# Polysketch attention followed by a rational-Padé feed-forward: keys in nine tiles of four, the first loads regrouped, one bank for the key-value products, and a new order of steps

## The chip, the cores and the metric

The kernel runs on one core of a Trainium2 chip. The metric is device time in microseconds (us): 277.58 us is the median of three runs (276.32 to 277.84). Beside these there is one profiled execution, whose trace is read below. The core has a matrix engine (TensorE, PE in the profile), a vector engine (VectorE, DVE), a scalar engine (ScalarE, ACT), GpSimd (POOL) and SyncE (SP), which here only issues DMA transfers. Each engine takes its instructions strictly in program order and waits on semaphores for what other engines and the transfers have to deliver.

## The reference, cut to what matters

Two stages. The first is a linear attention over 4 batches, 4 heads, 1088 tokens and head size 32, with two sketch matrices `S1` and `S2` of 8 x 32. The second is a feed-forward over all 4352 tokens (128 to 2048 to 128) with a rational function in the middle.

```python
def phi(x):
    a = einsum('rd,bhsd->bhsr', S1, x); b = einsum('rd,bhsd->bhsr', S2, x)
    return einsum('bhsi,bhsj->bhsij', a, b).reshape(..., 64)
q_p, k_p = phi(q), phi(k)
kv = einsum('bhsf,bhsd->bhfd', k_p, v); z = sum(k_p, axis=2)
x = einsum('bhsf,bhfd->bhsd', q_p, kv) / (einsum('bhsf,bhf->bhs', q_p, z) + 1e-6)

h = x @ w_in                                  # x as 4352 x 128
P = a0 + a1*h + a2*h**2 + a3*h**3
Q = 1 + |b0|*|h| + |b1|*h**2
out = (P / (Q + 1e-6)) @ w_out
```

The sums over tokens in `kv` and `z` take tokens in any order, so how the tokens of `k` and `v` are dealt out to tiles is free as long as both are dealt out alike.

## The kernel before, in words

**The table.** The program is a list of small steps. `ORDER` holds `name:index` entries; the loop at its end calls one method for each, and that call issues the instructions of the step, on one engine mostly. So the table sets the order on every engine at once, and nothing rearranges it later. Three loads are steps too: `lk`, `lv`, `lq` fetch the keys, values and queries of a later batch. All loads of batch 0 and of the weights are issued before the table begins.

**Keys.** For each batch, `Keys` makes `kv` and `z`. The 1088 tokens of a head lie as 32 groups of `NJ` = 34 tokens, one group to a partition, four heads on 128 partitions. `kt` (`transposes`) turns 32 x 32 blocks on VectorE so that a tile of 128 columns holds 4 x 32 tokens; `ks` (`sketches`) multiplies each tile by both sketch matrices on TensorE; `kc` (`copies`) takes one of the two results out of PSUM on ScalarE; `kf` (`features`) makes the 64 products on VectorE; `kp` (`products`) accumulates them against `v` and a column of ones on TensorE; `kk` (`keep`) copies the sums to `kvz` on ScalarE. Before, 34 = 4 * 8 + 2: eight full tiles (`NT`, `NM` = 8, 4) and a ninth of 64 tokens, in two parts of 4 and 5 tiles, with three transposes (512, 512 and 64 columns), and a `v` that takes six loads a batch: four of 128 KB and two of 16 KB.

**Queries.** `qt`, `qs`, `qc`, `qf`, `qp`, `qd`, `qi`, `qx`, `qb`, `qk` do a block of up to 384 queries: transposes, sketches, copies, features, products against `kvz`, denominator, its inverse, quotient, transposition back, and the copy to `xT`. Blocks 0 to 2 (batch 0) keep all on the chip. Blocks 3 to 12 (`Spread`) send their sketches through DRAM to spread them over partitions: `qc` copies them to `sk_sb`, then SP writes `sk_d` and reads back `a_all` and `b_all`, and `qf` on VectorE waits for that.

**Feed-forward.** Seventeen units of 4096 columns. Unit 0 is the first 256 tokens against all 16 blocks of hidden rows; each later tile of 512 tokens is two units. Of a unit, `h0` to `h3` are its hidden matmuls (TensorE, two PSUM tiles of 1024 columns in turn), `e0` to `e3` their copies to bf16 on ScalarE, `u`, `w`, `y` make Q on VectorE, `ln` and `ex` its reciprocal `r` on ScalarE, `pa` or `pd` the upper part of P on ScalarE or VectorE, `s`, `m`, `x` on VectorE build `h*r` and the rest, `G` multiplies by `w_out`, and `st` stores. `w_out` exists in three bf16 copies, made by six steps `wo:0` to `wo:5` (two halves of rows each); five ran on ScalarE and one on VectorE. Unit 0's `h2` and `h3` stand first in the table, and they need hidden blocks 8 to 15, the upper half of `w_in`. A step `tn` issues matmuls on an idle tile that produce nothing used.

**What stands around the change.** SP issues in program order; a load that waits for its buffer, or for room in the queue, holds all behind it. `k_sb` and `v_sb` have a single buffer: `lk:1` waits for the transposes of batch 0, `lv:1` for its products. PSUM has four banks for the attention (`bank`) and two tiles of two banks for the hidden layer (`wide`).

Of the kernel before, what the change touches and what calls it, by code (L numbers as in the profile page):

```python
# [11 lines left out]
FP = mybir.dt.float32  # L12
# [7 lines left out]
TURNS = (12, 2, 2, 2, 2, 2)  # L20
ORDER = """
tn:3 tn:0 kt0:0 kt2:0 kt1:0 ks0:0 qt:0 ba:0 tn:4 qt:1 kc0:0 tn:5 kf0:0 ks1:0 lk:1 qs:0 kc1:0 kf1:0 qc:0 kp0:0 qf:0
kp1:0 lv:1 qs:1 kk:0 qt:3 qc:1 qp:0 qt:2 qf:1 qs:3 qd:0 qs:2 qi:0 qx:0 qc:2 lq:1 qf:2 qp:1 qc:3 qb:0 qp:2 qd:1 qk:0
qi:1 qx:1 h2:0 wo:0 qd:2 wo:3 qi:2 qx:2 wo:4 h3:0 e2:0 wo:2 kt1:1 qb:1 h1:0 kt2:1 kt0:1 e3:0 wo:1 u1:0 ks1:1 w1:0
pa1:0 lk:2 qt:5 ks0:1 qt:4 qs:5 y1:0 h0:0 kc0:1 qk:1 kc1:1 wo:5 kf0:1 e1:0 kf1:1 qb:2 qs:4 qk:2 e0:0 h1:1 qt:6 ln1:0
qf:3 lq:2 u0:0 h2:1 w0:0 qc:4 ex1:0 kt0:2 tn:2 y0:0 qp:3 e2:1 s1:0 kp0:1 ln0:0 kt1:2 kp1:1 kt2:2 qt:7 m1:0 qd:3 e1:1
h0:1 qi:3 ex0:0 qx:3 x1:0 h3:1 e0:1 s0:0 kk:1 lk:3 h2:2 m0:0 lv:2 e3:1 pa0:0 u1:1 h3:2 w1:1 e2:2 ks0:2 y1:1 e3:2 h0:2
pa1:1 h1:2 qf:4 e0:2 x0:0 qp:4 kc0:2 qc:5 e1:2 kf0:2 ln0:1 ks1:2 pd0:1 u1:2 tn:1 qb:3 qd:4 G0:0 ex0:1 qi:4 w1:2 G1:0
qx:4 G2:0 qk:3 s0:1 kc1:2 ln1:1 qb:4 G3:0 y1:2 G4:0 qk:4 ex1:1 G5:0 kf1:2 qs:7 h2:3 ln0:2 qt:8 s1:1 h3:3 e2:3 m0:1
ex0:2 m1:1 h0:3 kt1:3 e3:3 qf:5 G0:1 s0:2 qs:8 qc:7 e0:3 h1:3 ln1:2 x0:1 st:0 h0:4 m0:2 e1:3 pa0:2 u1:3 h1:4 qt:9 w1:3  # L30
e0:4 G1:1 ex1:2 x1:1 h3:4 y1:3 e1:4 qp:5 e3:4 h2:4 x0:2 qd:5 ln0:3 lq:3 s1:2 qs:6 e2:4 G2:1 qi:5 pd1:2 ex0:3 G3:1 qx:5
u1:4 G4:1 G5:1 pa0:3 m1:2 qb:5 w1:4 G0:2 ln1:3 G1:2 qf:7 G2:2 m0:3 G3:2 qk:5 qc:6 ex1:3 x1:2 G4:2 h0:5 pd0:4 pa1:3
y1:4 h2:5 e0:5 qt:11 v0:3 ln0:4 kp0:2 s0:3 h3:5 m1:3 e2:5 ex0:4 x0:3 h1:5 v1:3 e3:5 kp1:2 s1:3 e1:5 s0:4 lv:3 h1:6
ln1:4 u1:5 h2:6 m0:4 e1:6 ex1:4 w1:5 G5:2 h0:6 kt0:3 kk:2 qf:6 e2:6 y1:5 G0:3 pa1:4 G2:3 h3:6 s1:4 ln0:5 st:2 qp:7
x1:3 e0:6 m1:4 qp:6 ex0:5 x0:4 G3:3 qc:8 s0:5 e3:6 G5:3 qd:7 ks0:3 qd:6 pa0:5 u1:6 G0:4 qi:6 qx:6 G1:4 qi:7 ln1:5 qx:7
G2:4 x1:4 qb:7 G3:4 w1:6 ex1:5 G4:4 m0:5 qb:6 qk:7 G5:4 qk:6 s1:5 pa0:6 qs:9 h0:7 y1:6 pa1:5 h1:7 kt2:3 m1:5 e0:7 G0:5
v0:5 kc0:3 e1:7 m0:6 h2:7 ln0:6 qf:8 h3:7 x1:5 qc:9 e2:7 st:4 qp:8 x0:5 e3:7 ex0:6 u1:7 ks1:3 h3:8 qt:10 w1:7 qd:8
ln1:6 qi:8 h1:8 y1:7 e3:8 kc1:3 ex1:6 G2:5 kf1:3 h0:8 e1:8 pd1:6 kf0:3 ln0:7 qs:10 h2:8 s1:6 e0:8 s0:6 G3:5 ex0:7 G4:5
m1:6 G5:5 qf:9 G0:6 qx:8 qc:10 e2:8 ln1:7 s0:7 qb:8 kp0:3 u1:8 kp1:3 qk:8 ex1:7 v0:6 G0:7 w1:8 h3:9 pa0:7 x0:6 y1:8
h2:9 kk:3 e3:9 G2:6 e2:9 s1:7 h1:9 ln0:8 m0:7 x1:6 h0:9 e1:9 m1:7 ex0:8 h0:10 x0:7 e0:9 u1:9 G3:6 ln1:8 pd1:7 G4:6  # L40
u0:9 G5:6 s0:8 e0:10 qp:9 qf:10 ex1:8 w1:9 qp:10 x1:7 pa0:8 h2:10 m0:8 w0:9 qd:9 qd:10 pa1:8 h1:10 qi:9 qt:12 qi:10
qx:9 y0:9 G1:7 e1:10 qb:9 s1:8 ln0:9 G2:7 G3:7 x0:8 h3:10 qk:9 qx:10 ex0:9 m1:8 qb:10 y1:9 G4:7 e3:10 G5:7 x1:8 qk:10
e2:10 h2:11 pd0:9 ln1:9 u1:10 h1:11 e2:11 w1:10 ex1:9 s0:9 h0:11 y1:10 e1:11 qs:11 G0:8 e0:11 h3:11 qc:11 s1:9 ln0:10
m0:9 h3:12 e3:11 m1:9 pa1:9 G1:8 u1:11 G2:8 x0:9 ex0:10 qs:12 G0:9 w1:11 h2:12 e3:12 s0:10 ln1:10 y1:11 G3:8 G1:9
e2:12 G4:8 ex1:10 x1:9 G2:9 pd0:10 h0:12 pa1:10 m0:10 s1:10 h1:12 ln0:11 x0:10 G5:8 qf:11 G3:9 m1:10 qc:12 ex0:11
qp:11 pd0:11 e0:12 G4:9 s0:11 qd:11 ln1:11 G5:9 qi:11 x1:10 G0:10 e1:12 qx:11 G1:10 m0:11 pa1:11 qb:11 G2:10 st:6
G3:10 u1:12 qk:11 G4:10 ex1:11 x0:11 h1:13 w1:12 pa0:12 h2:13 y1:12 e1:13 G5:10 e2:13 s1:11 h2:14 ln0:12 m1:11 h3:13
st:10 e2:14 st:8 ex0:12 qf:12 h3:14 x1:11 e3:13 qp:12 s0:12 e3:14 u1:13 h0:13 ln1:12 m0:12 w1:13 h0:14 qd:12 e0:13
qi:12 x0:12 ex1:12 G0:11 u0:13 qx:12 h1:14 w0:13 pa1:12 y1:13 qb:12 y0:13 G1:11 e0:14 G2:11 s1:12 e1:14 G3:11 ln0:13
u1:14 G4:11 m1:12 G5:11 ex0:13 G0:12 w1:14 G1:12 pd0:13 qk:12 ln1:13 h1:15 s0:13 y1:14 ex1:13 G0:13 h0:15 m0:13 e1:15  # L50
ln0:14 h3:15 x1:12 s1:13 e0:15 pd1:13 e3:15 h2:15 m1:13 ex0:14 x0:13 G2:12 e2:15 x1:13 G3:12 pa0:14 h2:16 u1:15 s0:14
G4:12 e2:16 w1:15 G5:12 ln1:14 G1:13 m0:14 h3:16 ex1:14 y1:15 G2:13 e3:16 h1:16 s1:14 ln0:15 u2:16 u3:16 h0:16 w2:16
x0:14 ex0:15 st:12 G3:13 pd0:15 e0:16 G4:13 y2:16 e1:16 G5:13 s0:15 ln1:15 G0:14 u0:16 G1:14 m0:15 G2:14 ex1:15 w0:16
G0:15 x0:15 G1:15 pa1:14 s1:15 G2:15 y0:16 G3:15 G4:15 m1:14 ln0:16 G3:14 m1:15 ex0:16 pd1:15 v1:14 w3:16 ln2:16 x1:15
ex2:16 x1:14 G5:15 pa2:16 y3:16 s0:16 G5:14 pa0:16 s2:16 G0:16 m0:16 ln3:16 G1:16 m2:16 ex3:16 x0:16 pa3:16 s3:16
G2:16 x2:16 G3:16 m3:16 G4:16 st:14 G5:16 G6:16 x3:16 G7:16 G8:16 st:16
""".split()
W_ENG = (0, 1, 1, 1, 1, 1)
P_ON_ACT = (1, 1, 0, 1, 1, 0, 1, 1, 0, 1, 1, 1, 1, 0, 1, 0, 1, 1, 0, 1, 0, 1, 0, 1, 1, 1, 0, 0, 1, 1, 0, 0, 1, 1)
SPLIT_A = (0, 9, 13)  # L60
QUARTER = (16,)
WIDE_S = ()
WIDE_M = ()
WIDE_X = (5, 14)
WIDE_P = (1, 2, 10)
HORNER = (6, 7, 10, 12, 29)
@with_exitstack
def kernel(
# [24 lines left out]
    NT = 8  # L93
    NM = 4
    NL = NJ - NM * NT
    assert 0 < NL <= 4

# [39 lines left out]
    kw = NM * W
    for x, eng in enumerate((nc.sync, nc.scalar)):
        eng.dma_start(out=k0[:, 0:kw].rearrange("p (m x d) -> p x m d", m=NM, x=2)[:, x],
                      in_=k0_src[:, 0:kw].rearrange("p (m x d) -> p x m d", m=NM, x=2)[:, x])  # L140
    s_raw = []
    for i, (s_in, eng) in enumerate(((S1, nc.sync), (S2, nc.scalar))):
        t = consts.tile([128, D], FP, name=f"s_raw{i}")
        eng.dma_start(out=t, in_=bass.AP(tensor=s_in.tensor, offset=s_in.offset,
                                         ap=[[0, 16], [D, R], [1, D]]))
        s_raw.append(t)
    nc.sync.dma_start(out=k0[:, kw:S], in_=k0_src[:, kw:S])
    q0 = io.tile([128, S], FP, name="q_sb", bufs=1)
# [85 lines left out]
    class Keys:  # L234
        def __init__(self, b, k_sb, v_sb, first=False):
            self.b, self.dst, self.k_sb, self.v_sb = b, kvz[b % 2], k_sb, v_sb
            self.take = wide if first else bank
            self.ab, self.sk, self.k_p = {}, {}, {}

        def transposes(self, part):  # L240
            self.kT = kTs[0]
            half = NM * NT * 32
            hT = self.kT[:, 0:half].rearrange("p (t m g) -> p m t g", t=NT, m=NM)
            hk = self.k_sb[:, 0:half].rearrange("p (m t d) -> p m t d", t=NT, m=NM)
            if part < 2:
                nc.vector.transpose(out=hT[:, :, part * 4:part * 4 + 4], in_=hk[:, :, part * 4:part * 4 + 4])
            else:
                nc.vector.transpose(out=self.kT[:, half:S], in_=self.k_sb[:, half:])
# [432 lines left out]
```

## Time and profile before

| what | value |
|---|---|
| median of 3 runs | 277.58 us |
| profiled execution, its own time | 277.93 us |
| its span, first to last instruction | 276.1 us (1.8 us lie around it) |
| VectorE busy | 255.4 us, 92% |
| ScalarE busy | 250.6 us, 91% |
| TensorE busy, ends modelled | 260.7 us, 94% |
| VectorE busy from 40 to 260 us | 219.0 of 220 us |
| ScalarE busy from 40 to 260 us | 218.9 of 220 us |
| VectorE busy from 0 to 20 us | 10.3 us |
| DMA engines' mean busy share from 2 to 22 us | 0.88 to 1.15 |
| first hidden matmul | 19.31 us |
| first rational step on VectorE (`u1:0`) | 24.74 us |

The busy shares are averages over a start in which the engines wait for the loads, a long stretch in which VectorE and ScalarE are both full, and a short end. Where an engine is full from some moment on, the end of the span is that moment plus the work that is left on it.

### The profile page before, as it was taken

Reading aid. Unit: us, or ns where it says so; the run is one execution under the profiler, and the core shown is the slowest. Engines: PE = TensorE matmul, PEld = TensorE weight load, DVE = VectorE, ACT = ScalarE, POOL = GpSimd, SP = SyncE. Lnnn points to the kernel's source line nnn. Section 1 sums busy time; section 2 is a strip of 40 time slices with the busy share of each in tenths; the row PEclk is TensorE's granted clock in tenths of the full one; section 3 lists DMA queues with packets and bytes.
Section 4 is the critical chain, followed back from the end, with each engine's and each line's share of the span. In section 5 each row is a group of like instructions: output and inputs, shape, how many; then the busy total and the mean of one; then the engine's idle time right before and its main releaser. Section 6 shows DMA issues by size and latency. Waiting matters only on the chain.

```text
span 276.1 us, 3618 instructions
## 1 busy us (share of the span) xinstructions
PE 260.7 (94%) x1326; PEld 137.9 (50%) x1326; DVE 255.4 (92%) x278; ACT 250.6 (91%) x230; POOL 2.9 (1%) x24
## 2 busy tenths in 40 slices
PE   7999998999999999999999999999999998999482
PEld 2888464674454546546364554344545433444130
DVE  2666699999999999999999999999999999999992
ACT  1259979999999999999999999999999999999980
POOL 3000000000000000000000000000000000000000
PEclk9999999999999999999999999999999999999888
DMA  6994848040520332301413000040324000002005
GB/s 161 238 292 117 228 140 183 16 114 9 141 81 12 97 81 38 95 36 60 85 42 90 1 0 2 14 114 0 101 47 69 7 0 0 2 7 32 0 0 77
DMA packets 30481, 19.53 MB, mean 71 GB/s; under 512 B 21504, under 2 KB 25856, under 8 KB 30464
## 3 DMA queue, kind: packets, MB, share of 16 engines
q1 hardware_dynamic: 28304, 18.64, 27.7%
q10 hardware_dynamic: 2160, 0.68, 1.1%
q8 instruction: 10, 0.16, 0.3%
q14 instruction: 7, 0.06, 0.1%
HBM read 16.16 MB, written 3.15 MB: 70 GB/s over the span
## 4 chain that ended last, share of the span: by engine, by line
ACT 59%; DVE 16%; issue 10%; DMA 8%; PE 4%; SPq 1%; ACTq 0%; DVEq 0%
ACT ln L523 16%; ACT hh L438 15%; ACT r L527 14%; ACT p L518 9%; DMA w_out_sb_f<-in_moe_w_out_dram 4%; DVE w L472 3%; DVE s L531 3%; PE att_ps L565 3%; DVE g L546 2%; DVE w L467 2%; DMA b_all<-sk_d 2%; DVE g L535 2%; DVE u L461 2%; DMA k_sb<-in_k_dram 2%; PE h_ps L432 1%
## 5 line engine op out<-in xcount | busy, mean ns | idle before, releaser
L432 PE MATMUL h_ps<-xT,w_in_sb 128*128 128x512 f32 (+1 forms) x288 | 126.1, 577 | 2.7 <-ACT hh L438 1.7
L432 PEld LDWEIGHTS h_ps<-xT,w_in_sb 128*128 128x128 f32 x288 | 52.5, 190 | 56.8 <-issue 41.2
L438 ACT CAST hh<-h_ps 128x1024 bf16<-128x1024 f32 x68 | 69.3, 1043 | 0.1
L523 ACT ACTIVATE ln<-w 128x2048 f32<-128x2048 bf16 (+1 forms) x35 | 66.6, 1904 | 2.4 <-DVE w L472 2.3
L565 PEld LDWEIGHTS <-w_out 128*128 128x128 bf16 x412 | 40.4, 99 | 54.3 <-issue 19.8
L527 ACT ACTIVATE r<-ln 128x2048 bf16<-128x2048 f32 (+1 forms) x35 | 66.5, 1899 | 0.3
L518 ACT ACTIVATE p<-hh,a_sb 128x2048 bf16<-128x2048 bf16 (+1 forms) x23 | 46.9, 2049 | 0.0
L531 DVE TENSOR_TENSOR s<-hh,r 128x2048 bf16<-128x2048 bf16 (+1 forms) x35 | 41.2, 1185 | 0.5 <-ACT r L527 0.3
L565 PE MATMUL att_ps<-g,w_out 128*128 128x512 bf16 (+1 forms) x144 | 36.5, 380 | 5.0 <-DVE g L546 5.0
L472 DVE TENSOR_TENSOR w<-w,u 128x4096 bf16<-128x4096 bf16 (+2 forms) x22 | 39.4, 1795 | 0.1
L535 DVE TENSOR_TENSOR g<-hh,s 128x2048 bf16<-128x2048 bf16 (+1 forms) x30 | 35.1, 1177 | 0.1
L546 DVE TENSOR_TENSOR g<-g,p 128x2048 bf16<-128x2048 bf16 (+1 forms) x30 | 35.2, 1175 | 0.0
L565 PE MATMUL att_ps<-r,w_out 128*128 128x512 bf16 (+1 forms) x144 | 35.1, 368 | 0.0
L565 PE MATMUL att_ps<-s,w_out 128*128 128x512 bf16 (+1 forms) x124 | 29.8, 365 | 0.0
L467 DVE TENSOR_SCALAR w<-u,b_abs 128x4096 bf16<-128x4096 bf16 (+2 forms) x22 | 24.1, 1094 | 0.1
L461 DVE TENSOR_SCALAR u<-hh 128x4096 uint16<-128x4096 uint16 (+2 forms) x22 | 21.4, 975 | 0.7 <-ACT hh L438 0.7
L346 PEld LDWEIGHTS att_ps<-kvz,q_pT 128*128 128x128 f32 x144 | 17.5, 192 | 4.1 <-issue 1.9
L346 PE MATMUL att_ps<-kvz,q_pT 128*128 128x66 f32 x144 | 17.7, 273 | 0.2
L410 DVE TENSOR_TENSOR q_pT<-a_all,b_all 128x768 f32<-128x768 f32 (+1 forms) x10 | 8.9, 886 | 2.5 <-DMA b_all<-sk_d 2.5
L285 PEld LDWEIGHTS att_ps<-v_sb,k_p 128*64 128x64 f32 (+1 forms) x288 | 9.1, 137 | 2.4 <-issue 2.0
L285 PE MATMUL att_ps<-v_sb,k_p 128*64 128x64 f32 (+1 forms) x288 | 10.1, 225 | 0.0
L513 DVE TENSOR_SCALAR p<-hh,a_sb 128x2048 bf16<-128x2048 bf16 x12 | 9.6, 796 | 0.0
(59 smaller groups left out, 138.8 us busy)
## 6 DMA issues: line engine op xcount, KB each, us to landing
a_all<-sk_d SPq DMA_DIRECT2D x6, 384.0 KB, 3.8
b_all<-sk_d SPq DMA_DIRECT2D x12, 192.0 KB
v_sb<-in_v_dram SPq DMA_DIRECT2D x16, 128.0 KB, 5.7
k_sb<-in_k_dram SPq DMA_DIRECT2D x3, 544.0 KB
q_sb<-in_q_dram SPq DMA_DIRECT2D x3, 544.0 KB
a_all<-sk_d SPq DMA_DIRECT2D x4, 320.0 KB
b_all<-sk_d SPq DMA_DIRECT2D x8, 160.0 KB
out_dram<-out_sb SPq DMA_DIRECT2D x18, 64.0 KB, 1.9
```

Source lines behind the costliest of these rows:

```text
L346: nc.tensor.matmul(self.nd[:, o:o + 2 * KW], lhsT=self.q_p[:, c, x:x + 128], rhs=kvz[self.b % 2][:, c, :], start=True, stop=True)
L432: nc.tensor.matmul(t[:, x * tl:(x + 1) * tl], lhsT=w_in_sb[:, f * 128:(f + 1) * 128], rhs=xT[:, t0:t0 + tl], start=True, stop=True)
L438: nc.scalar.copy(out=live[i]["hh"][:, part * PW:(part + 1) * PW], in_=live[i]["h", part])
L467: nc.vector.tensor_scalar(out=t[:, c], in0=live[i]["u"][:, c], scalar1=ab1, scalar2=ab0, op0=AX.mult, op1=AX.add)
L472: nc.vector.tensor_mul(out=t[:, c], in0=t[:, c], in1=live[i]["u"][:, c])
L518: nc.scalar.activation(out=part_of(i, "p", h), in_=hh, func=ACT.Identity, scale=a3, bias=a2)
L523: nc.scalar.activation(out=t, in_=live[i]["w"][:, span(h)], func=ACT.Ln, bias=1.0 + 1e-6)
L527: nc.scalar.activation(out=part_of(i, "r", h), in_=live[i]["ln"], func=ACT.Exp, scale=-1.0)
L531: nc.vector.tensor_mul(out=part_of(i, "s", h), in0=hh, in1=part_of(i, "r", h))
L535: nc.vector.tensor_mul(out=part_of(i, "g", h), in0=hh, in1=part_of(i, "p" if horner(i, first(h)) else "s", h))
L546: nc.vector.tensor_mul(out=g, in0=g, in1=part_of(i, "s" if horner(i, first(h)) else "p", h))
L565: nc.tensor.matmul(outs[t0][:, :tl], lhsT=w_sb[y][:, f0 + x, :], rhs=part_of(i, key, h)[:, c:c + tl], start=done[0] == 0, stop=done[0] == ...
```

## The change

It does the following.

- **Keys in nine tiles of four.** `NT` becomes 9: 34 = 3 * 9 + 7, so every tile has its first three blocks of 32 tokens, and the fourth block is there in seven of the nine tiles. `v` then takes four loads a batch (three of 144 KB, one of 112 KB). For later batches the transposes are two (864 and 224 columns). Batch 0 has three parts (2, 2 and 5 tiles) and four transposes (256, 256, 480 and 96 columns).
- **The first loads.** `k` of batch 0 comes in three pieces, two on SP and a small one on ScalarE's queue; both sketch matrices go first on ScalarE's queue; the first half of `q` moves to SP, `a` and `b` to GpSimd's queue. `w_out` becomes two half loads and `w_in` two (before: one and four), and with the rest of `q` they are steps of the table (`lw`, `lx`, `lq:0`). On SP the order after `v` is now: `w_out` first half, rest of `q`, `w_out` second half, upper half of `w_in`, `k` of batch 1, lower half of `w_in`, then `v` and `q` of batch 1. Before it was: all of `w_in`, rest of `q`, `w_out`, then `k`, `v`, `q` of batch 1.
- **One bank for k times v.** For later batches both pairs of heads accumulate in one PSUM bank; the products of both parts are issued together at `kp1`, and `kk` is two copies of two rows instead of four.
- **Fewer idle matmuls:** 19 instead of 22.
- **Constants.** One of the six `wo` steps moves from ScalarE to VectorE; the `s` steps of units 3 and 5 become one instruction of 4096 columns instead of two of 2048; one half of `p` on ScalarE is exchanged for another.
- **The table is written anew**, from the first step to the last.

The diff, without the table's rows and cut to its core:

```diff
-TURNS = (12, 2, 2, 2, 2, 2)
+TURNS = (9, 2, 0, 0, 2, 0, 2, 2, 2)
-W_ENG = (0, 1, 1, 1, 1, 1)
+W_ENG = (0, 0, 1, 1, 1, 1)
-WIDE_S = ()
+WIDE_S = (3, 5)
...
-    NT = 8
     NM = 4
-    NL = NJ - NM * NT
+    NT = -(-NJ // NM)
+    NL = NJ - (NM - 1) * NT
...
         for m in range(NM):
-            nc.sync.dma_start(out=t[m * 32:(m + 1) * 32, :, 0:W], in_=vv[:, :, m * W:(m + 1) * W])
-        for jj in range(NL):
-            c = (NM * NT + jj) * D
-            nc.sync.dma_start(out=t[jj * 32:(jj + 1) * 32, :, W:W + D], in_=vv[:, :, c:c + D])
+            w = min(W, (NJ - m * NT) * D)
+            nc.sync.dma_start(out=t[m * 32:(m + 1) * 32, :, 0:w], in_=vv[:, :, m * W:m * W + w])
...
-    for i, (s_in, eng) in enumerate(((S1, nc.sync), (S2, nc.scalar))):
+    for i, s_in in enumerate((S1, S2)):
...
-    nc.scalar.dma_start(out=a_sb, in_=bass.AP(tensor=moe_a.tensor, offset=moe_a.offset,
+    nc.gpsimd.dma_start(out=a_sb, in_=bass.AP(tensor=moe_a.tensor, offset=moe_a.offset,
...
-    for c in range(0, d_ff, 512):
-        nc.sync.dma_start(out=w_in_sb[:, c:c + 512], in_=moe_w_in[:, c:c + 512])
-    nc.sync.dma_start(out=q0[:, 512:S], in_=q0_src[:, 512:S])
...
-    nc.sync.dma_start(out=w_out_sb_f, in_=moe_w_out.rearrange("(fo fi) d -> fi fo d", fi=128))
...
+            if first:
+                self.PARTS = ((0, 2), (2, 2), (4, NT - 4))
+                self.BLOCKS = [[(slice(0, NM), slice(0, 2))], [(slice(0, NM), slice(2, 4))], [(a, slice(4, NT))], [(b, last)]]
+            else:
+                self.PARTS = ((0, 4), (4, NT - 4))
+                self.BLOCKS = [[(a, slice(0, NT))], [(b, slice(0, NL))]]
...
+            elif not self.first:
+                self.kv = bank()[:, 0:128].rearrange("p (c x) -> p c x", c=2)
...
+                    nc.scalar.copy(out=self.dst[p, :, a * KW:(a + 1) * KW], in_=self.kv[p, :, 0:KW])
...
+    def fetch_w(x):
+        f = slice(x * (nf // 2), (x + 1) * (nf // 2))
+        nc.sync.dma_start(out=w_out_sb_f[:, f], in_=w_out_src[:, f])
+
+    def fetch_x(x):
+        c = slice(x * (d_ff // 2), (x + 1) * (d_ff // 2))
+        nc.sync.dma_start(out=w_in_sb[:, c], in_=moe_w_in[:, c])
```

## The prediction

> **What bounds the kernel now.** I read the page's busy shares and slices first, then the table of stages, then the timeline of the first 40 us, then that of the end.
>
> From the page (the slices are 6.9 us each, digits are tenths):
>
> ```profile
> PE 260.7 (94%) x1326; PEld 137.9 (50%) x1326; DVE 255.4 (92%) x278; ACT 250.6 (91%) x230; POOL 2.9 (1%) x24
> ...
> DVE  2666699999999999999999999999999999999992
> ACT  1259979999999999999999999999999999999980
> ```
>
> From the table of stages (columns: PE, PEld, DVE, ACT, POOL busy, granted clock, DMA share, GB/s):
>
> ```profile
> 0.00:20.00 20.00, 17.71 (x165) 12.44 (x166) 10.28 (x25) 5.45 (x16) 2.92 (x24) 1.00 0.89 231
> 20.00:40.00 20.00, 19.45 (x158) 14.23 (x156) 15.19 (x23) 18.26 (x21) 0.00 (x0) 1.00 0.63 163
> 40.00:60.00 20.00, 18.95 (x103) 12.07 (x102) 19.79 (x20) 19.94 (x24) 0.00 (x0) 1.00 0.49 116
> ```
>
> From 40 us to the end of the last tile VectorE and ScalarE are both full, so the end is the moment at which they become full plus their work. What can be won lies in the first 40 us, where VectorE is idle for 14.5 us. The timeline shows on what it waits (in brackets, idle time before and its releaser):
>
> ```profile
> 15.00 0.84 DVE L306 STREAM_TRANSPOSE qT<-q_sb 128x320 f32<-128x320 f32 x2 [2.42 <-DMA q_sb<-in_q_dram]
> ...
> 19.31 3.67 PE L432 MATMUL h_ps<-xT,w_in_sb 128*128 128x256 f32 x16
> ...
> 19.77 0.75 DVE L602 TENSOR_SCALAR w_out<-w_out_sb_f,a_sb 128x1024 bf16<-128x1024 f32 x1 [0.46 <-DMA w_out_sb_f<-in_moe_w_out_dram]
> ...
> 22.61 0.71 DVE L246 STREAM_TRANSPOSE kT<-k_sb 128x512 f32<-128x512 f32 x1 [1.45 <-DMA k_sb<-in_k_dram]
> ...
> 24.74 0.69 DVE L461 TENSOR_SCALAR u<-hh 128x2048 uint16<-128x2048 uint16 x1 [0.70 <-ACT hh L438]
> ...
> 33.78 0.83 DVE L410 TENSOR_TENSOR q_pT<-a_all,b_all 128x640 f32<-128x640 f32 x1 [2.49 <-DMA b_all<-sk_d]
> ```
>
> To be seen: four waits on loads, then the first rational step u1:0 at 24.74, then 2.49 us lost to the DRAM round trip of query block 3. After that VectorE does not wait again for more than a few tenths.
>
> **The change part by part.** All sums go against the profiled execution: 277.93 us, of which 276.1 is the span.
>
> Loads. The DMA engines are full from 2 to 22 us, so landing times follow the bytes ahead in the queue. Before, the rest of q landed at 15.0 with 2.75 MB ahead and itself (k 0.56, q 0.26, v 0.56, w_in 1.05, rest of q 0.29, sketches 0.03): 211 GB/s from 2.0 us. w_out (1.05 MB) took 15.0 to 19.77, so 2.4 us a half; k of batch 1 (0.56 MB) 2.84 more. Now the first half of w_out has 1.93 MB: 2.0 + 1.93/0.211 = 11.1. Rest of q: 2.23 MB, 12.5. Second half of w_out 14.9. The upper half of w_in, 0.52 MB at the stage's 231 GB/s, 17.2; k of batch 1 20.0; lower half of w_in 22.3. Ends: the bytes up to the upper half of w_in are a part of what had landed by 19.77 before, so 19.8 is the late end; the early end is 16.0, at the best slices' 375 GB/s for that half and 2 us for w_out's. Likewise the lower half is in by 22.6, when before all of it and k of batch 1 had landed.
>
> Keys of batch 0. Before, the features ended at 11.55, the products at 13.63 and kk at 14.39. Now there is one part more on each engine: a copy (247 ns row against two of about 220), a feature step (1225 against two of about 690), a transpose: 0.5 us together. The sketches, issued first, land between 3.2 (1.25 plus the shortest landing in the page, 1.9) and 5.4 as before; I take 4. Part one can start about a microsecond earlier, so products end at about 13.0. wo:4 stands ahead of kk on ScalarE, 11.1 + 0.3 + 1.05 = 12.5, just in time. kk ends at 13.8.
>
> ScalarE up to the first hidden tile: after kk the copies of block 1 (0.59), wo:2 (1.15), copies of block 2 (0.65), wo:5 (1.05; its half landed at 14.9), xT (0.39): 13.8 + 3.83 = 17.6. VectorE's part runs beside it: rest of q 12.5, transposes 0.84, block 1's features after their copy at 14.4 to 15.1, denominator to quotient 0.78, transposed back by 16.4. So xT at 17.6 and w_in at 17.2 come together, and the hidden matmuls start at 17.6 instead of 19.31. They take 3.67, and the second copy ends at 22.3. In the trace ScalarE was busy with w_out parts when the tiles were ready (copies at 21.76 and 23.71); now only wo:3 stands there and is done by 19.1. u1:0 starts at 22.3: a gain of 2.4 us. Its ends are 0.2 (w_in at 19.8) and 3.5 (w_in at 16.0 and kk a microsecond earlier).
>
> VectorE's work after u1:0. The second wo on VectorE (0.75) runs before u1:0 in time in which it waited. Block 2's inverse and quotient now come after it: +0.62. Keys of batches 2 and 3: two transposes for three; from 696 ns at 512 columns and 221 at 64 a column costs 1.06 ns, so 1.07 + 0.39 against 1.61: -0.15 each, -0.3. Wide s: 2283 for twice 1216, -0.15 each, -0.3. Together 0.0. These forms are not in the trace; if a transpose split into three blocks of nine cost a block's start each (0.15), it would be +0.6 over both, if not -0.3, and I keep 0.3 each way.
>
> The wait for block 3. Its qf:0 now stands after m1:0, qt:5 and x1:0, the first tile's s and g, instead of ahead of u0:0. Counting VectorE's rows from 22.3, it comes up at about 36, against a landing at 33.78 before with the same bytes ahead. So 2.49 go. What is late next: qt:4 and qt:6 need q of batch 1 at 25.6 (no wait at 26.20 before), kf1:1 its copy on ScalarE at about 28.7. I take 0.4 for these, 0 to 2.0.
>
> ScalarE after its first hidden copy (21.76, now 19.5): three w_out parts fewer, 3.4 us; kk of three batches 4 x 181 against two copies of 2 x 33 columns, between 181 and 362 each, so 0 to 1.1, I take 1.0 by the short end, since 33 more columns cost ScalarE a few tens of ns (273 at 128 columns, 301 at 160). With the earlier start that is 6.5 us earlier, more than VectorE gains: ScalarE gets slack and VectorE sets the end.
>
> TensorE: three idle matmuls fewer (0.2 to 0.4 each) and no other change of count. Same steps in the tail: unit 16 and the stores end alike. Loads on GpSimd's queue: the next part.
>
> Sum: -2.4 + 0.0 - 2.49 + 0.4 = -4.5, with 277.93: 273.4. The profiled execution is 0.35 above the median of the runs shown, 277.58, which gives 273.1 on that scale.
>
> One rule speaks against the change, the matrix engine's clock. At the end of the trace a gap of 3.86 us is followed by matmuls at half pace (8 in 3.43 us, 0.43 from start to start, 0.216 elsewhere in groups of the same form):
>
> ```profile
> 260.91 3.43 PE L565 MATMUL att_ps<-g,w_out 128*128 128x512 bf16 x8 [3.86 <-DVE g L546]
> ```
>
> Before the first hidden tile TensorE now has less work and fewer idle matmuls from 14 to 17.6. If it falls to half pace there, the first 3.4 us of hidden matmuls do half their work, and u1:0 comes 1.7 later: 274.8. The Trainium skill (TensorE: Matmul & The Clock Gate, Part 1) says the clock comes back after about 3.4 us of steady work, whatever the number of matmuls; an estimate by that page gives the same 1.7. The trace's 3.4 us of half pace agree.
>
> **The rivals.**
>
> A gain of half the size. w_in lands near 19.8, or TensorE is cold: u1:0 gains 0.2 to 0.7 and the wait for block 3 still goes. -0.5 - 2.49 + 0.4 = -2.6, so 275.0 on the median's scale. For it: 512-byte pieces of w_out ahead of w_in, slower per byte than the mean. Against it: the bytes.
>
> No change. The gain of the start is given back: VectorE meets waits of 4 us in the long stretch, since every in-order neighbour is a new one. Each r it has to wait for costs up to 1.95 (a wide s needs both halves of r, so two such places), each DRAM round trip 2.5. Against it: ScalarE, which delivers r, runs 2 us ahead, and before there was under 1 us of such waits in 220. 277.5.
>
> Slower. a and b now come over GpSimd's queue, and the trace has no load from there. ba:0 on ScalarE needs b and stands ahead of the copies of block 0, wo:4, kk and all that follows. Up to 10.4 it is covered (block 0's sketches end then); beyond that every microsecond goes on to xT and u1:0. It decides above 10.4 + 4.5 = 14.9: b landing at 17.0 would give 279.7. Bounds from rows: the same load took 3.4 us from issue to landing on ScalarE's queue (4.90 to 8.32), the longest, w_out, 9.9; issued at about 1, that is 4.4 to 10.9. So it hardly reaches 14.9. The same queue's masks, now behind the two issues (0.33 to 0.82 each on the other queues), are needed at 4.3 and ready at 3.1. By the Trainium skill (DMA: Bandwidth & Descriptors, Latency and other measured facts) first bytes of such a load come after about 1 us; no row here shows it.
>
> **How the numbers follow.** This kernel's runs spread by 0.5%, so less than 0.5% (1.4 us) can't be told from no change. Forecast -4.5: 0.55. Half the gain: 0.21. No change: 0.10. Slower: 0.14 (0.06 for GpSimd's loads, 0.08 for waits in the long stretch that exceed the gain by over 1.4). So faster 0.76, same 0.10, slower 0.14. The likeliest time is 273.1. Low: u1:0 at its early end (-1.1 more), no new waits (-0.4), a shorter transpose (-0.3) make 271.3, and 0.8 for ScalarE's slack: 270.5. High: the half gain and no change are inside, and 278.4 leaves the slower case's larger half out.
>
> **What would show it.** u1:0 (u on the first tile) near 22.3; the first hidden matmul near 17.6 with w_out's parts before it; block 3's features without a wait; VectorE full from there, ScalarE with idle time that names VectorE. Wrong if the first hidden matmul comes after 19.8, if VectorE's idle time after 36 us is over 2 us, if hidden matmuls run at double their step, or if b_abs comes after 10.4.

## The result, and the profile after

The changed kernel takes 279.06 us (median of 8 runs, 278.77 to 279.92), the kernel before in the same rounds 277.31 us (8 runs, 276.32 to 277.87). The ratio is 1.007, with an interval of 1.005 to 1.009: slower by 1.75 us where 4.5 less were forecast. The profiled execution took 279.01 us, its span is 277.2 us; before these were 277.93 and 276.1.

From the page of the changed kernel: busy times, then slices of 6.9 us in tenths, the last line the granted TensorE clock, that is the share of its full clock at which TensorE was let run.

```profile
PE 262.4 (95%) x1308; PEld 138.8 (50%) x1323; DVE 255.8 (92%) x276; ACT 250.0 (90%) x224; POOL 4.2 (2%) x26
...
DVE  1656999999999999999999999999999999999992
ACT  1157999998999999999999999999999999999990
PEclk9689999999999999999999999999999999999898
```

The long stretch is as full as before. What is new lies in the start: TensorE's clock is at 6 and 8 tenths in the second and third slice, VectorE does less in the first and third (1 for 2, 5 for 6), and ScalarE in the second and fourth (1 for 2, 7 for 9).

The table of stages of the changed kernel (PE, PEld, DVE, ACT, POOL busy, granted clock, DMA share, GB/s):

```profile
0.00:20.00 20.00, 16.74 (x131) 11.02 (x133) 7.88 (x18) 5.28 (x13) 4.20 (x26) 0.83 0.80 231
...
5.30:8.71 3.41, 1.34 (x8) 0.76 (x7) 2.12 (x9) 0.21 (x1) 1.08 (x4) 1.00 0.90 218
8.71:12.13 3.42, 3.42 (x16) 2.92 (x16) 2.12 (x4) 0.61 (x3) 0.00 (x0) 0.50 1.13 309
12.13:15.54 3.41, 3.41 (x25) 2.23 (x25) 1.10 (x2) 0.00 (x0) 0.00 (x0) 0.50 1.07 379
...
40.00:260.00 220.00, 214.61 (x1036) 109.11 (x1049) 218.88 (x218) 217.23 (x184) 0.00 (x0) 1.00 0.22 55
```

From 40 to 260 us VectorE works 218.9 us (before 219.0) and ScalarE 217.2 (218.9). From 8.71 to 15.54 us TensorE is busy throughout, at half its clock. Read in slices of a quarter of a microsecond, the clock falls at 8.71 and rises at 15.54: 6.83 us.

The timeline of the changed kernel (start, duration, in brackets the idle time before and its releaser):

```profile
1.20 4.56 PE L169 MATMUL att_ps<-idle 128*128 128x512 bf16 x11 [1.20 <-DVE idle L164]
...
4.03 0.21 DVE L194 STREAM_TRANSPOSE sT<-s_raw 128x32 f32<-128x32 f32 x1 [2.90 <-DMA s_raw<-in_S_dram]
...
6.59 0.21 DVE L194 STREAM_TRANSPOSE sT<-s_raw 128x32 f32<-128x32 f32 x1 [2.34 <-DMA s_raw<-in_S_dram]
...
7.76 3.78 PE L256 MATMUL h_ps<-S,kT 128*128 128x64 f32 x18 [2.01 <-DVE kT L250]
...
11.33 1.91 PE L169 MATMUL att_ps<-idle 128*128 128x512 bf16 x4
...
13.18 1.12 PE L297 MATMUL att_ps<-v_sb,k_p 128*64 128x64 f32 x16
14.23 1.76 PE L333 MATMUL h_ps<-qT,SAB 64*128 64x256 f32 x8
...
14.42 0.69 DVE L268 TENSOR_TENSOR k_p<-h_ps,b_sk 128x512 f32<-128x512 f32 x1 [1.88 <-PE att_ps L297]
15.92 1.85 PE L297 MATMUL att_ps<-v_sb,k_p 128*64 128x64 f32 x56
...
22.89 3.72 PE L446 MATMUL h_ps<-xT,w_in_sb 128*128 128x256 f32 x16
...
27.69 0.69 DVE L475 TENSOR_SCALAR u<-hh 128x2048 uint16<-128x2048 uint16 x1 [2.19 <-ACT hh L452]
...
41.33 0.82 DVE L424 TENSOR_TENSOR q_pT<-a_all,b_all 128x640 f32<-128x640 f32 x1
```

And the same stretch before:

```profile
1.19 4.89 PE L172 MATMUL att_ps<-idle 128*128 128x512 bf16 x14 [1.19 <-DVE idle L167]
...
6.67 1.10 PE L256 MATMUL h_ps<-S,kT 128*128 128x64 f32 x8 [0.59 <-DVE kT L246]
...
7.61 1.03 PE L172 MATMUL att_ps<-idle 128*128 128x512 bf16 x4
```

To be seen, in order. The eleven idle matmuls end at 5.76. The first sketch matrix is used as it lands, at 4.03, but the sketches need both, and the second lands at 6.59. So TensorE stands idle for 2.01 us (0.59 before). From 8.71 on its work takes up to twice its time: four idle matmuls 1.91 us against 1.03, the query sketches of block 0 1.76 against 1.13. Only the last products, from 15.92, run at full pace again. Apart from these 2.01 us TensorE's matmuls have no wait of 0.2 us or more until the first hidden matmul: its own queue of work fills the start. The first hidden matmul comes at 22.89 (19.31 before), and `u1:0` at 27.69 (24.74), 2.95 later. Everything after that is shorter: from `u1:0` to the end of the span it was 251.4 us and is 249.5, 1.9 less; the feature step of query block 3, which had waited 2.49 us, now runs at 41.33 without a wait. 2.95 − 1.9 is the 1.1 us by which the span grew.

### The profile page after: what moved, and what is told of

It reads as the page before. It is cut to its first block, busy times and chain, and to the rows that moved or that the text cites. A ratio compares the mean times of both kernels' runs of the same rounds, so it can differ in the third digit from the quotient of the medians.

```text
span 277.2 us, 3567 instructions
## 1 busy us (share of the span) xinstructions
PE 262.4 (95%) x1308; PEld 138.8 (50%) x1323; DVE 255.8 (92%) x276; ACT 250.0 (90%) x224; POOL 4.2 (2%) x26
## 4 chain that ended last, share of the span: by engine, by line
DVE 33%; ACT 28%; PE 24%; issue 12%; DMA 2%; ACTq 0%; DVEq 0%
PE h_ps L446 12%; ACT ln L537 7%; ACT hh L452 7%; ACT r L541 7%; DVE g L549 6%; DVE s L545 6%; DVE w L486 4%; DVE g L560 4%; ACT p L532 4%; PE att_ps L579 4%; DVE w L481 3%; DVE u L475 3%; PE att_ps L360 2%; DMA s_raw<-in_S_dram 2%; DVE out_sb L588 1%
## 5 line engine op out<-in xcount | busy, mean ns | idle before, releaser
L452 ACT CAST hh<-h_ps 128x1024 bf16<-128x1024 f32 x68 | 68.1, 1024 | 3.2 <-PE h_ps L446 2.8
L537 ACT ACTIVATE ln<-w 128x2048 f32<-128x2048 bf16 (+1 forms) x35 | 65.8, 1879 | 0.2
L545 DVE TENSOR_TENSOR s<-hh,r 128x2048 bf16<-128x2048 bf16 (+2 forms) x33 | 40.9, 1245 | 0.1
L579 PE MATMUL att_ps<-g,w_out 128*128 128x512 bf16 (+1 forms) x139 | 34.9, 373 | 3.0 <-DVE g L560 2.7
L579 PE MATMUL att_ps<-r,w_out 128*128 128x512 bf16 (+1 forms) x138 | 34.5, 374 | 1.2 <-ACT r L541 0.8
```

Source lines behind the costliest of these rows:

```text
L452: nc.scalar.copy(out=live[i]["hh"][:, part * PW:(part + 1) * PW], in_=live[i]["h", part])
L537: nc.scalar.activation(out=t, in_=live[i]["w"][:, span(h)], func=ACT.Ln, bias=1.0 + 1e-6)
L545: nc.vector.tensor_mul(out=part_of(i, "s", h), in0=hh, in1=part_of(i, "r", h))
L579: nc.tensor.matmul(outs[t0][:, :tl], lhsT=w_sb[y][:, f0 + x, :], rhs=part_of(i, key, h)[:, c:c + tl], start=done[0] == 0, stop=done[0] == ...
```

## The experiments

What had to be told apart: that TensorE's clock, lost in the gap behind the idle matmuls, makes the start slow; that the feature buffers do (the ring holds two, and there are three parts: the third feature step waits 1.88 us at 14.42); that loads on GpSimd's queue, or the new order of the first loads, do. "Rest" below is the time from `u1:0` to the end of the span. Ratios are against the kernel before, whose medians were 277.2 us in each of the three sets of rounds.

**The idle matmuls alone: nine more of them.** The first number of `TURNS` and two more are issued ahead of the sketches: 11 in the changed kernel, 20 here.

```diff
-TURNS = (9, 2, 0, 0, 2, 0, 2, 2, 2)
+TURNS = (18, 2, 0, 0, 2, 0, 2, 2, 2)
```

> The changed kernel with 20 idle matmuls ahead of the first sketches instead of 11, nothing else. Theory clock: in the changed kernel TensorE stood idle for 2.0 us (5.76 to 7.76) and the granted clock was 0.50 from 9 to 15 us, which stretched the sketches (3.78 us for 18), the four idle matmuls (1.91), the first products and block 0's sketches. With no gap the clock stays at 1.00, u1:0 comes at about 24 instead of 27.7, and the time is about 275.3, 1.4% less than the changed kernel's 279.1. Theory sketch matrices (they land at 6.59 instead of 5.38, and that is the delay): u1:0 moves by less than 0.5 us, about 279. Theory feature buffers (the third feature step waits for the first products): 278 to 279.

Measured: 275.82 us (275.68 to 276.05, 4 runs), ratio 0.9938 (0.9923 to 0.9953). Its timeline and table of stages:

```profile
5.91 0.21 DVE L194 STREAM_TRANSPOSE sT<-s_raw 128x32 f32<-128x32 f32 x1 [1.69 <-DMA s_raw<-in_S_dram]
...
7.91 2.24 PE L256 MATMUL h_ps<-S,kT 128*128 128x64 f32 x18
...
9.99 1.03 PE L169 MATMUL att_ps<-idle 128*128 128x512 bf16 x4
...
24.41 0.69 DVE L475 TENSOR_SCALAR u<-hh 128x2048 uint16<-128x2048 uint16 x1 [2.19 <-ACT hh L452]
```

```profile
5.30:8.71 3.41, 3.41 (x19) 1.98 (x18) 2.28 (x8) 0.21 (x1) 1.08 (x4) 1.00 1.05 243
8.71:12.13 3.42, 3.42 (x38) 2.64 (x39) 2.92 (x4) 0.61 (x4) 0.00 (x0) 1.00 1.13 291
12.13:15.54 3.41, 3.41 (x71) 2.64 (x67) 1.35 (x3) 2.06 (x6) 0.00 (x0) 1.00 1.07 381
```

The sketches start even later than in the changed kernel (7.91 for 7.76), but 18 instructions take 2.24 us instead of 3.78, the clock is full throughout, and `u1:0` comes 3.28 us earlier. That is half of 6.83 within 0.14. Rest is 249.5, the same, and it is the same without the half pace that the changed kernel also has near its end (from 261.30 to 264.71; none here until 272.3): lost there, the clock costs nothing. Nine matmuls on data that nobody reads turn a loss of 0.7% into a gain of 0.6%.

**The feature buffers: a third one.** The second part's features go into columns of `xT` that are written only later.

```diff
-            k_p = self.k_p[part] = tmp.tile([128, 5, H, R, R], FP, name="k_p")
+            if self.first and part == 1:
+                k_p = xT[:, n_tok - 512:].rearrange("p (t h i j) -> p t h i j", t=2, h=H, i=R)
+            else:
+                k_p = tmp.tile([128, 5, H, R, R], FP, name="k_p")
+            self.k_p[part] = k_p
```

> The changed kernel with a third buffer for the feature step of part two of batch 0 (in the columns of xT that are written last), so that it need not wait for the first products. Theory feature buffers: VectorE's wait of 1.88 us at 14.4 goes and u1:0 comes 1 to 1.9 us earlier, 277.2 to 278. Theory clock: the products of parts two and three stand behind block 0's sketches on TensorE (done at 16.0), so an earlier feature step moves nothing: 279, clock 0.50 from 9 to 15 us as before.

Measured: 278.80 us (276.95 to 280.38, 10 runs), ratio 1.005 (1.0022 to 1.0077). The feature step waits no more, and the time stays within the spread of the runs. In the profiled run, the slowest of the ten, the second sketch matrix was later still, and so was everything:

```profile
8.16 0.21 DVE L194 STREAM_TRANSPOSE sT<-s_raw 128x32 f32<-128x32 f32 x1 [3.75 <-DMA s_raw<-in_S_dram]
...
9.33 3.96 PE L256 MATMUL h_ps<-S,kT 128*128 128x64 f32 x18 [3.26 <-DVE kT L250]
```

So the wait of 1.88 us follows from slow products and does not cause the loss. Here, too, the clock is at half for 6.83 us, from 9.74 to 16.57.

**The same loss in the kernel before: six idle matmuls fewer.**

```diff
-TURNS = (12, 2, 2, 2, 2, 2)
+TURNS = (6, 2, 2, 2, 2, 2)
```

> The kernel before with 8 idle matmuls ahead of the first sketches instead of 14, nothing else. Theory clock: they end near 4.6, the sketches start at 6.7 as before, the gap of 2 us drops the clock to 0.50 as in the changed kernel, u1:0 comes about 3 us later, and the time is about 280, 1% more than before. If the clock is not the cause: 277.3.

Measured: 278.61 us (278.32 to 280.74, 10 runs), ratio 1.0065 (1.0041 to 1.0088). Taking idle matmuls from the old kernel costs 1.4 us, about half of what was expected and nearly as much as the whole change. Its timeline and one line of its stages (this profiled run was the second longest of the ten):

```profile
1.19 3.59 PE L172 MATMUL att_ps<-idle 128*128 128x512 bf16 x8 [1.19 <-DVE idle L167]
...
7.13 1.97 PE L256 MATMUL h_ps<-S,kT 128*128 128x64 f32 x8 [2.35 <-DVE kT L246]
...
8.90 1.91 PE L172 MATMUL att_ps<-idle 128*128 128x512 bf16 x4
...
29.12 0.69 DVE L461 TENSOR_SCALAR u<-hh 128x2048 uint16<-128x2048 uint16 x1 [2.68 <-ACT hh L438]
```

```profile
8.00:10.00 2.00, 2.00 (x9) 1.35 (x9) 1.01 (x3) 0.47 (x2) 0.00 (x0) 1.00 0.82 152
```

Four idle matmuls in 1.91 us are half pace, as in the changed kernel, although the clock's column says 1.00 here. The eight at the start are all 0.43 apart: this run had not come to full pace when they ended, so here the clock was not lost but never gained. By its spacing TensorE stays at half pace until about 17 (the query sketches of block 0 take 2.08 us for 1.13, the products 3.48 for 2.46). Spacing is the surer witness. `u1:0` is 4.38 us later than before, yet the span only 2.6 longer: Rest is 249.6 instead of 251.4, because query block 3's features, at 35.59, now have nothing to wait for. So part of the loss is hidden here, and that its size is near that of the whole change is partly chance.

The reverse, four idle matmuls more in the kernel before:

```diff
-TURNS = (12, 2, 2, 2, 2, 2)
+TURNS = (16, 2, 2, 2, 2, 2)
```

> The kernel before with 18 idle matmuls ahead of the sketches instead of 14, nothing else. Theory clock: the kernel before was warm already, so more of them win nothing: 277.0 to 277.5. If idle matmuls help by themselves (a warmer TensorE anywhere later): 275 to 276.

Measured: 277.21 us (276.25 to 279.05, 12 runs), ratio 0.9996 (0.9971 to 1.0021). The old kernel had enough of them; more win nothing.

**Loads on GpSimd's queue: `a` and `b` back to ScalarE's.** The two statements change only the engine that issues.

```diff
-    nc.gpsimd.dma_start(out=a_sb, in_=bass.AP(tensor=moe_a.tensor, offset=moe_a.offset,
+    nc.scalar.dma_start(out=a_sb, in_=bass.AP(tensor=moe_a.tensor, offset=moe_a.offset,
...
-    nc.gpsimd.dma_start(out=b_sb, in_=bass.AP(tensor=moe_b.tensor, offset=moe_b.offset,
+    nc.scalar.dma_start(out=b_sb, in_=bass.AP(tensor=moe_b.tensor, offset=moe_b.offset,
```

> The changed kernel with a and b loaded from ScalarE's queue, behind the last piece of k, instead of GpSimd's. Theory sketch matrices held up by GpSimd's loads: the second sketch matrix lands at 4 to 5.4 us instead of 6.59, the gap on TensorE falls under 1 us, its clock stays up, u1:0 at about 24, 275 to 276. Theory that the bulk loads on SP hold it up: it lands at about 6.6 again, 279. Theory clock says only that the time follows the gap on TensorE.

Measured: 275.03 us (274.72 to 278.20, 10 runs), ratio 0.9941 (0.9905 to 0.9978). The profiled run:

```profile
5.10 0.21 DVE L194 STREAM_TRANSPOSE sT<-s_raw 128x32 f32<-128x32 f32 x1 [0.77 <-DMA s_raw<-in_S_dram]
...
6.27 2.50 PE L256 MATMUL h_ps<-S,kT 128*128 128x64 f32 x18 [0.21 <-DVE kT L250]
```

I had priced this edit by the landing of `b`; it acts on another load. The second sketch matrix lands at 5.10 instead of 6.59, the gap shrinks to 0.21, and the clock holds. But not in every run, and the mean granted clock of each run goes with its time:

```
us     274.72 274.73 274.80 274.90 274.95 275.10 276.16 277.73 277.75 278.20
clock  0.990  0.987  0.998  0.998  0.987  0.999  0.982  0.978  0.984  0.977
```

3.41 us at half clock are 0.006 of this mean, and a run can have such a stretch in its tail too, which blurs it without moving the time (the fastest runs here have 0.990 and 0.987); still, the four longest runs have the four lowest means. That eleven idle matmuls end too near the landing to hold the clock each time fits; there is no trace of one of these longer runs to show it.

The same edit the other way round, in the kernel before (`a` and `b` from ScalarE's queue to GpSimd's):

```diff
-    nc.scalar.dma_start(out=a_sb, in_=bass.AP(tensor=moe_a.tensor, offset=moe_a.offset,
+    nc.gpsimd.dma_start(out=a_sb, in_=bass.AP(tensor=moe_a.tensor, offset=moe_a.offset,
...
-    nc.scalar.dma_start(out=b_sb, in_=bass.AP(tensor=moe_b.tensor, offset=moe_b.offset,
+    nc.gpsimd.dma_start(out=b_sb, in_=bass.AP(tensor=moe_b.tensor, offset=moe_b.offset,
```

> The kernel before with only a and b moved to GpSimd's queue. If GpSimd's loads hold up the sketch matrices, these land 0.5 to 2 us later than 5.4, the gap on TensorE grows from 0.6 to 1 to 2.5 us, and runs with a cold TensorE appear: 277.5 to 279. If not: 277.2, first transposition at 5.4.

Measured: 277.16 us (276.29 to 278.81, 12 runs), ratio 1.0001 (0.9979 to 1.0023).

```profile
6.24 0.30 DVE L197 STREAM_TRANSPOSE sT<-s_raw 128x32 f32<-128x32 f32 x2 [5.10 <-DMA s_raw<-in_S_dram]
...
7.53 1.10 PE L256 MATMUL h_ps<-S,kT 128*128 128x64 f32 x8 [1.34 <-DVE kT L246]
8.47 1.03 PE L172 MATMUL att_ps<-idle 128*128 128x512 bf16 x4
```

There, too, the sketch matrices came later (6.24 for 5.38), and the gap grew to 1.34 us, but with 14 idle matmuls ahead the clock held (four in 1.03 us), and no time was lost. With 14 idle matmuls the queue is no loss; with eleven, by the run before this one, it is.

**The order of the first loads.** In the changed kernel, one sketch matrix first on SP's queue, the other first on ScalarE's, ahead of `k`:

```diff
+    for i, (s_in, eng) in enumerate(((S1, nc.sync), (S2, nc.scalar))):
...
+        eng.dma_start(out=t, in_=bass.AP(tensor=s_in.tensor, offset=s_in.offset,
...
-    for i, s_in in enumerate((S1, S2)):
...
-        nc.scalar.dma_start(out=t, in_=bass.AP(tensor=s_in.tensor, offset=s_in.offset,
```

> The changed kernel with the first sketch matrix first on SP's queue and the second first on ScalarE's, instead of both on ScalarE's; a and b stay on GpSimd's queue and the idle matmuls stay 11. Theory that a small load issued behind the start of the bulk loads is what lands late: both land by 4.2, the sketches wait for k (5 to 5.5) instead, the gap on TensorE stays under 0.5 us, clock up, 274.5 to 275.5. Theory that GpSimd's two small loads are what holds the second matrix up: it lands after 5.5 again, and the time lies between 275 and 279.

Measured: 278.56 us (278.37 to 278.88, 11 runs), ratio 1.0053 (1.0035 to 1.0071).

```profile
3.22 0.30 DVE L194 STREAM_TRANSPOSE sT<-s_raw 128x32 f32<-128x32 f32 x2 [2.08 <-DMA s_raw<-in_S_dram]
...
6.11 1.63 DVE L250 STREAM_TRANSPOSE kT<-k_sb 128x256 f32<-128x256 f32 x4 [2.27 <-DMA k_sb<-in_k_dram]
...
6.93 0.66 PE L256 MATMUL h_ps<-S,kT 128*128 128x64 f32 x4 [1.75 <-DVE kT L250]
...
10.84 1.91 PE L169 MATMUL att_ps<-idle 128*128 128x512 bf16 x4
```

Both matrices land at 3.2, but now `k` is late, the gap is 1.75 us, and TensorE runs at half pace as before. The sketches start 0.8 us sooner than in the changed kernel, and `u1:0` comes 0.8 us sooner, at 26.87: what is won is the earlier start alone. The gap costs here too, though another load makes it.

In the kernel before, both sketch matrices first on ScalarE's queue (the statements also move ahead of the loads of `k`):

```diff
-    for i, (s_in, eng) in enumerate(((S1, nc.sync), (S2, nc.scalar))):
+    for i, (s_in, eng) in enumerate(((S1, nc.scalar), (S2, nc.scalar))):
```

> The kernel before with only the sketch matrices moved to the front of ScalarE's queue, as in the change. Theory that the second of two small loads there lands late whatever else is done: it lands at 5.5 to 6.6, the sketches of part one start later than 6.7, 277.3 to 278.5. If it lands by 4.5 here, with GpSimd's queue unused, GpSimd's loads were the cause in the changed kernel, and the time is 276.5 to 277.3.

Measured: 277.47 us (276.48 to 279.72, 12 runs), ratio 1.0009 (0.9985 to 1.0034): no difference. The matrices land at 4.00 and 5.02, the sketches start at 6.16 for 6.67, and `u1:0` is at 25.26: here the start of the sketches was not what the end waited for. TensorE waits later instead, 1.20 us for VectorE at 10.36. The second matrix's landing lies between the two that were expected, so this run does not settle what delays it.

**Both remedies in the changed kernel.** Twenty idle matmuls and `a`, `b` on ScalarE's queue (the two diffs above together):

> The changed kernel with 20 idle matmuls ahead of the sketches and with a and b on ScalarE's queue: both of the edits that each gave about 275. Theory clock, with the second sketch matrix's landing as what opens the gap: the gap is now closed from both ends, so every run should be warm: 274.6 to 275.2 with none near 278, u1:0 at 23.5 to 24.4. If the two edits removed separate losses, 272 to 273.

Measured: 275.34 us (275.09 to 276.04, 6 runs), ratio 0.9934 (0.9909 to 0.9960). `u1:0` is at 23.91, 0.5 earlier than with the idle matmuls alone: but the sketches now wait for the idle matmuls to end (7.41). With sixteen (the kernel of sixteen below):

```diff
-TURNS = (9, 2, 0, 0, 2, 0, 2, 2, 2)
+TURNS = (14, 2, 0, 0, 2, 0, 2, 2, 2)
```

> The changed kernel with 16 idle matmuls ahead of the sketches, ending near 6.4, and a and b on ScalarE's queue. The 20 of the run before ended at 7.4 and held the sketches back by half a microsecond. Theory clock: no gap above 2 us even when the second matrix comes late, sketches at about 6.4, u1:0 near 23.7, 274.7 to 275.1, no run near 278. Rival (the gap is not what decides): 275 to 278 in two groups, as with 11 idle matmuls.

Measured: 275.17 us (274.75 to 275.48, 6 runs), ratio 0.9911 (0.9882 to 0.9939), sketches at 6.49, `u1:0` at 23.37, and none of the runs is above 275.5. Of its timeline:

```profile
6.49 2.49 PE L256 MATMUL h_ps<-S,kT 128*128 128x64 f32 x18 [0.28 <-DVE kT L250]
...
14.56 0.59 ACT L340 COPY a_all<-h_ps 128x512 f32<-128x512 f32 x1 [0.58 <-PE h_ps L333]
...
16.65 0.65 ACT L343 COPY a_all<-att_ps 128x256 f32<-128x256 f32 x2 [0.45 <-PE att_ps L333]
...
16.97 0.44 PE L386 MATMUL att_ps<-ident,x_tok 128*128 128x128 f32 x2
...
17.53 1.11 PE L360 MATMUL att_ps<-kvz,q_pT 128*128 128x66 f32 x8
...
18.57 3.72 PE L446 MATMUL h_ps<-xT,w_in_sb 128*128 128x256 f32 x16
...
23.37 0.69 DVE L475 TENSOR_SCALAR u<-hh 128x2048 uint16<-128x2048 uint16 x1 [2.19 <-ACT hh L452]
```

ScalarE waits 0.58 and 0.45 us for the query sketches of blocks 1 and 2, which stand behind the products on TensorE. TensorE's matmuls have no wait of 0.2 us or more from 6.49 until the hidden matmuls at 18.57.

The same without the four idle matmuls between sketches and products:

```diff
-TURNS = (14, 2, 0, 0, 2, 0, 2, 2, 2)
+TURNS = (14, 2, 0, 0, 0, 0, 0, 2, 2)
```

> The same with the four idle matmuls between the sketches and the first products left out. Theory that v's landing at about 10.1 sets the first products: they start at about 10.1 as before, 274.6 to 275.1, and the wait on TensorE of about 1.4 us stays under the 1.7 that was harmless. Theory that the idle matmuls set them: 0.3 to 0.5 faster. If a gap of 1.4 us there cools TensorE: 277 to 278.

Measured: 275.34 us (274.77 to 276.77, 10 runs), ratio 0.9935 (0.9909 to 0.9962). Six runs lie from 274.8 to 275.5 with mean clocks of 0.993 to 0.998, four at 276.6 to 276.8 with 0.991 to 0.993. The profiled run is one of the four; its timeline and a line of its stages:

```profile
10.03 0.69 PE L297 MATMUL att_ps<-v_sb,k_p 128*64 128x64 f32 x16 [1.17 <-DMA v_sb<-in_v_dram]
10.65 2.06 PE L333 MATMUL h_ps<-qT,SAB 64*128 64x256 f32 x8
```

```profile
11.00:13.00 2.00, 2.00 (x14) 1.19 (x14) 0.51 (x1) 0.26 (x1) 0.00 (x0) 0.50 1.16 332
```

A wait of 1.17 us for `v` went with a clock at half from 10.71 to 14.12, for 3.41 us, and `u1:0` fell to 25.06, 1.69 later than in the kernel of sixteen: half of 3.41. Six of the ten runs, by their times and means, did not lose it. The harmless 1.7 us of the expectation stands in no trace: of the gaps at the start the longest that kept the clock was 1.34, and 1.75 lost it.

Last, that kernel of sixteen with `wo:5` moved behind `wo:3`, out of ScalarE's way to `xT`:

```diff
-qs:2 qd:0 qc:2 qi:0 qx:0 wo:5 qs:3 qf:2 qb:0 qp:1 wo:1 qk:0 qc:3 wo:3 wo:0 h2:0
+qs:2 qd:0 qc:2 qi:0 qx:0 qs:3 qf:2 qb:0 qp:1 wo:1 qk:0 qc:3 wo:3 wo:5 wo:0 h2:0
```

> The same as the first of these with the step wo:5 on ScalarE behind the copy of block 0 to xT instead of ahead of it. In the changed kernel the transposition of block 0 was done 0.7 us before ScalarE came free of wo:5. If xT sets the first hidden matmul: it starts 0.7 us earlier, u1:0 too, 274.0 to 274.4. If w_in sets it: no change, 274.7 to 275.1.

Measured: 274.79 us (274.38 to 275.36, 6 runs), ratio 0.9899 (0.9867 to 0.9931). It is the fastest of all, 2.4 us under the kernel before, though not to be told from the kernel of sixteen: `xT`'s copy starts at 17.64 instead of 18.13, but the first hidden matmul at 18.67 instead of 18.57, so the step was not what held it. Neither expected reason fits: in both kernels the hidden matmuls follow at once on the products of block 1 (17.73 here, 17.53 there), which TensorE has to do before them.

## Why the prediction was wrong, point by point

**The step that failed** is the start: "Part one can start about a microsecond earlier, so products end at about 13.0", together with "TensorE: three idle matmuls fewer (0.2 to 0.4 each) and no other change of count". I took the first sketch matrix's landing (4, measured 4.03) for both; the second came at 6.59. And I priced idle matmuls as work saved, when in this kernel they hold the clock until the first operands are there. The path was wrong with it: I summed ScalarE's instructions up to `xT`, while the first hidden matmul comes when TensorE's own queue is done. That queue has no wait of 0.2 us from 7.76 to 22.89 in the changed kernel, so a slower clock goes in full into `u1:0`; and in the last run `xT` half a microsecond sooner brought the hidden matmul no sooner. Products ended at 17.8 instead of 13.0, and at 13.5 in the kernel of sixteen.

**The miss in numbers.** `u1:0` was forecast at 22.3 and came at 27.69, 5.4 late. Adding nine idle matmuls took off 3.28: the clock. From there to the kernel of sixteen another 1.04: the late second sketch matrix, and more idle matmuls than needed while waiting for it. The last 1.07, from 23.37 to 22.3, is the path: the kernel of sixteen ends `kk` at 13.98, against 13.8 forecast, and has `xT` at 18.5 instead of 17.6, as ScalarE waits 0.58 and 0.45 for TensorE, which the forecast's sum of ScalarE's instructions (3.83) left out. But `xT` half a microsecond sooner won nothing (the last run): TensorE goes from the sketches of block 1 at 13.38 through its queue with no wait of 0.2 us, and is free for the hidden matmuls at 18.57, not at 17.6.

**The clock was named, at the wrong place and size.** The forecast looked for a cold TensorE, one at half its clock, from 14 to 17.6 and gave it 1.7 us, one stretch of 3.4 us at half pace. It was cold from 8.7, for 6.83 us, and cost 3.3. The Trainium skill (TensorE: Matmul & The Clock Gate, Part 1) describes an activity window of about 3.4 us that runs freely, and a change after at least one idle or one busy window. The lengths measured here, 3.41 and 6.83, agree with the window. That a gap of 2.01 us sufficed does not agree with a whole idle window, and the clock took two windows to come back although TensorE was busy for all of the first; the measurement decides.

**What was right.** All that comes after `u1:0`: forecast −2.49 + 0.4 + 0.0 = −2.1, measured −1.9. VectorE's work after `u1:0` grew by 0.35 us (0.0 forecast), and its idle time fell by 2.2. Block 3's wait went, VectorE has under 1.2 us idle from 40 to 260, ScalarE has gained slack (217.2 of 220). The changed kernel alone does not prove this: the old kernel with eight idle matmuls, as late as it, has a Rest of 249.6 and no such wait either. What shows it is that with `u1:0` at 23.4 to 24.4, sooner than before, Rest stays at 249.5 to 249.8 without the wait. The gap at the start hid a gain that was there.

**The loads** came sooner than the 211 GB/s of the forecast: the DMA engines, at 324 to 412 GB/s from 10 to 16 (read in stretches of 2 us), had the first loads behind them at about 17: their share is 0.70 from 16 to 17 and 0.20 from 17 to 18. No wait for `w_in` shows.

**The rivals.** "Half the gain" had the mechanism, a cold TensorE, but with too small a price. "No change" fell: no new waits in the long stretch. "Slower" named GpSimd's queue, but by `b` landing after 14.9; `b` landed at about 7.2. `b_abs` did come after 10.4, at 11.69, as ScalarE was itself behind TensorE. Taking the edit that it named back removes the loss in most runs, but by way of the second sketch matrix. Of the signs by which the forecast was to be wrong, two showed: `b_abs`, and the first, the hidden matmul after 19.8.

## What to carry to other kernels

Matmuls on unread data at the start are not spare work: count them so that they last until the first real operand has landed in its latest run, and leave the clock no gap on the way to the next load. When an edit changes what lands first, move the end of the idle matmuls with it. And price a lost clock by what TensorE has to do in the whole stretch at half pace, not by the length of the gap, and only where its work is what the rest waits for: here 2.0 us of idling at the start cost 3.3, and 3.41 us of half pace near the end cost nothing.

## What the runs showed of the hardware that was not expected

- **Half pace comes in lengths of 3.41 us.** Falls and rises of the granted clock, read in quarter-microsecond slices: 8.71 to 15.54 in the changed kernel, 9.74 to 16.57 with the third feature buffer, 7.57 to 14.41 with the sketch matrices first on two queues (6.83 each, twice 3.41), 10.71 to 14.12 without the second group of idle matmuls (3.41). The moments differ from run to run. In the third of these the idle matmuls' weight loads go from 0.43 us apart to closer at 4.16, which is 3.41 before the fall at 7.57: rise and fall lie on one grid. Why one kernel loses one length at the start and the others two is open; in those with two, TensorE was busy for all or nearly all of the first. With eight idle matmuls in the old kernel half pace lasted longer still, by its spacing from the first matmul to about 17.
- **How short a gap is enough** has no sharp bound: at the start 0.59, 1.20 and 1.34 us kept the clock, 1.75, 2.01 and 3.26 lost it, and 1.17 lost it in the kernel without the second group. Near the end the traces hold a cleaner comparison: in nine of them TensorE has one and the same gap of 2.72 or 2.73 us, between the same instructions. Four keep the clock (for one, the kernel of twenty idle matmuls, first line), five lose it for 3.41 us (for one, the kernel of sixteen, second line). So the length of a gap does not decide; that its place on the grid does fits, and was not tested by itself.

```profile
257.17 1.02 PE L579 MATMUL att_ps<-g,w_out 128*128 128x512 bf16 x4 [2.72 <-DVE g L560]
256.14 1.40 PE L579 MATMUL att_ps<-g,w_out 128*128 128x512 bf16 x4 [2.73 <-DVE g L560]
```

- **The first idle matmuls run at half pace**, 0.43 us apart, for 2.5 to 5 us from 1.19 on (in the kernel of eight, all of them), and the clock's column says 1.00 there. In the changed kernel all eleven are: they were about the number that it takes to come to full pace at all.
- **A small load behind large ones lands late, and not always alike.** The second 16 KB sketch matrix, issued at about 1.4, was used at 5.91, 6.59 and 8.16 in three runs with two small loads (2 KB and 1 KB) on GpSimd's queue, and at 5.10 to 5.31 in five runs of the changed kernel's variants with those on ScalarE's; the first, in all of these, at 3.99 to 4.20. That the two loads are the cause fits, also with 5.38 and 6.24 in the kernel before; by what way they delay it was not tested.
